# The second layer of a fused attention and bilinear MLP kernel: seven block products in place of eight

## The chip, the cores and the metric

The kernel runs on one core of a Trainium2 chip. The metric is device time in microseconds (us) of one launch; the times given are medians of several launches. Engines are called by the profile's names: PE (TensorE matmuls) and PEld (its weight loads), DVE (VectorE), ACT (ScalarE), POOL (GpSimd) and SP (SyncE, which here only issues transfers).

## The reference, cut to what matters

```python
def _attn_ref(q, k, v, w_pre, w_post):            # q, k, v: 4 x 12 x 448 x 64
    scores = np.matmul(q, k.transpose(0, 1, 3, 2)) / np.sqrt(64)
    scores = np.einsum('bhij,hg->bgij', scores, w_pre)
    attn = softmax(scores)                        # over the last axis
    attn = np.einsum('bhij,hg->bgij', attn, w_post)
    return np.matmul(attn, v)

def _moe_ref(x, w_a, w_b, w_out):                 # x: 1792 x 768, w_a, w_b: 768 x 1536, w_out: 1536 x 768
    return ((x @ w_a) * (x @ w_b)) @ w_out
```

The weights arrive as 64-bit floats and q, k, v as 32-bit floats; the result is float32.

## The kernel before

The attention takes the first 366 us or so and is not touched. Its result x stands transposed in DRAM, one block of 768 x 448 for each batch b (b = 0 to 3).

**First layer** (h = (x w_a) * (x w_b)), from about 366 to 705 us. The outer loop runs over f = 0 to 11, each f being 128 of the 1536 inner columns, and the inner loop over b. A step (f, b) is `run_a` and then `run_b`: each is 6 blocks of 128 rows of x, with three matmuls a block (high weights by high x, high weights by low x, low weights by high x; L583 to L585), since float32 is computed as sums of parts that the matmul takes in fp32r. `take_a` copies the first product from PSUM on ACT (L589), `take_b` multiplies the second by it on DVE into hf (L595) and stores hf to the DRAM tensor hd (L596, on SP, a step later).

In the same steps the weights of a later f, and those of the second layer, are converted from 64 to 32 bits: `bits` is six DVE instructions over 768 columns (L518 to L523) and one POOL addition (L524). For w_a and w_b, `split` then makes the high part on ACT (L561) and the low part on POOL (L562), into a pair of tiles wh and wl; for w_out, `conv_o` stores the converted block to the DRAM tensor wod (L550). `order` lists the conversions and `todo` says in which step (f, b) each runs.

**Second layer** (h w_out), from 705 us to the end. The loop runs over b and, inside it, over m = 0 to 5, the blocks of 128 output columns. A step j = (b, m) loads its weights from wod (`load_o`, two steps ahead), splits them (`split_o`: 2 ACT casts and 2 POOL subtractions of 768 columns), multiplies 12 blocks by three matmuls (`mm3`, L572 to L574), copies the result from PSUM on ACT with a change of order (L641 twice, L646) and stores it (L647). The h of the next b is loaded by three transfers at m = 0 (`load_h`, L624) and split at m = 2 to 5, 12 casts on ACT (L629) and 12 subtractions on DVE (L630). The first h is loaded after step (11, 1) of the first layer, and split in steps (11, 2) and (11, 3), six blocks each.

Instructions on an engine run in the order in which the program writes them, and SP issues its transfers in that order; buffers rotate inside a pool's tag (`bufs`). The tag `s` has two buffers (x of b = 0 and 1, later h), as has `pt` (attention weights, later x of b = 3 and h); PSUM products of the second layer take in turn `m` (three buffers) and `p0` or `p1` (one each).

Of the kernel before, what the change touches and what calls it, by code (L numbers as in the profile page):

```python
# [21 lines left out]
def talking_heads_bilinear_kernel(  # L22
# [20 lines left out]
    AB = 5  # L43
# [87 lines left out]
    def later(fn, n=3):  # L131
        todo_at.setdefault(now[0] + n, []).append(fn)
# [281 lines left out]
    for c in range(1, NC):  # L414
        b, t0, _ = chunks[c]
# [110 lines left out]

    def to_f32(u):
        t = raws.pop(u)
        n = mo["m"] = mo.get("m", -1) + 1
        m = (mo["w"] if n % 3 == 2 else mc).tile([128, CW], I32, tag="m", name="cvm", bufs=1 if n % 3 == 2 else 2)  # L530
        r = mc.tile([128, CW], I32, tag="r", name="cvr", bufs=1)
        return m.rearrange("p (k f) -> p k f", k=KD), bits(t[:, :, 0], t[:, :, 1], m, r)

    def conv_f(u):
# [7 lines left out]

        return ops, parts

    def conv_o(u):
        kind, i, e = u
        m, ops = to_f32(u)

        def store():
            nc.sync.dma_start(out=wod[:, i, e * KD:(e + 1) * KD], in_=m.bitcast(F32))  # L550

        return ops, lambda: later(store, 2)

    def load_o(j):
        if j < B * KD:
            raws["o", j] = raw_space().rearrange("p (k f) -> p k f", f=128)
            nc.sync.dma_start(out=raws["o", j], in_=wod[:, j % KD])

    def split(hh, ll, raw, e):
        sl = slice(e * KD, (e + 1) * KD)  # L560
        nc.scalar.copy(hh[:, sl], raw)  # L561
        nc.gpsimd.tensor_tensor(ll[:, sl], raw, hh.bitcast(F32)[:, sl], op=ALU.subtract)  # L562

    def split_o(j):
        hh, ll = new_w(("o", j))
        raw = raws.pop(("o", j))
        for e in range(2):
            split(hh, ll, raw[:, e * KD:(e + 1) * KD], e)

    def mm3(o, hh, ll, mh, ml, n, k0=0):  # L570
        for kk in range(n):
            nc.tensor.matmul(o, lhsT=hh[:, k0 + kk], rhs=mh[:, kk], start=(kk == 0), stop=False)  # L572
            nc.tensor.matmul(o, lhsT=hh[:, k0 + kk], rhs=ml[:, kk], start=False, stop=False)  # L573
            nc.tensor.matmul(o, lhsT=ll[:, k0 + kk], rhs=mh[:, kk], start=False, stop=(kk == n - 1))  # L574

    sas = {}

# [9 lines left out]
    def take_a(f, b, pa):  # L587
        sa = sb_p.tile([128, S], F32, tag="sb0", name="sa")
        nc.scalar.copy(sa, pa)  # L589
        sas[f, b] = sa  # L590

    def take_b(f, b, pb):
        sa = sas.pop((f, b))
        hf = w_p.tile([128, S], F32, tag="an", name="hf", bufs=AB)
# [8 lines left out]
    def run_b(f, b):  # L603
        pb = ps.tile([128, 512], F32, tag=f"p{b % 2}", name="pb", bufs=1)[:, :S]
        product(f, b, 1, pb, 0, KD)
        take_b(f, b, pb)
# [8 lines left out]
        if k1 == KD:  # L615
            (take_b if e else take_a)(0, 0, o)

    ht = {}

    def load_h(b):  # L620
        ll = big.tile([128, KF, S], F32R, tag="s" if b % 2 == 0 else "pt", name="hl")
        hh = big.tile([128, KF, S], F32R, tag="s" if b % 2 == 0 else "pt", name="hh")
        for f0, f1 in ((0, KF // 2), (KF // 2, KF - 1), (KF - 1, KF)):
            nc.sync.dma_start(out=ll.bitcast(F32)[:, f0:f1], in_=hd[b][:, f0:f1])  # L624
        ht[b] = (hh, ll)

    def split_h(b, f):
        hh, ll = ht[b]
        nc.scalar.copy(hh[:, f], ll.bitcast(F32)[:, f])  # L629
        nc.vector.tensor_tensor(ll[:, f], ll.bitcast(F32)[:, f], hh.bitcast(F32)[:, f], op=ALU.subtract)  # L630

    def run_o(j):
        b, m = divmod(j, KD)
        hh, ll = wt.pop(("o", j))
        th, tl = ht[b]
        po = ps.tile([128, 512], F32, tag="m" if j % 2 == 0 else f"p{j // 2 % 2}", name="po", bufs=3 if j % 2 == 0 else 1)[:, :S]
        mm3(po, hh, ll, th, tl, KF)
        so = sb_p.tile([128, S], F32, tag="sb1", name="so")
        n = S // QU * QU
        for e in range(2):  # L640
            nc.scalar.copy(  # L641
                so[:, :n].rearrange("p (u j e t) -> p u j e t", j=2, e=2, t=QH)[:, :, :, e],
                po[:, :n].rearrange("p (u e j t) -> p u e j t", j=2, e=2, t=QH)[:, :, e],
            )
        if n < S:
            nc.scalar.copy(so[:, n:], po[:, n:])  # L646
        nc.sync.dma_start(out=out[m * 128:(m + 1) * 128, b * S:(b + 1) * S], in_=so)  # L647

    order = [("f", f, e) for f in range(3) for e in range(2)] + [("o", 0, 0), ("o", 0, 1)]
    for f in range(2, KF):  # L650
# [86 lines left out]
    with tc.manual_schedule():  # L737
# [117 lines left out]
        fin3()  # L855
        todo = {(1, b): order[4 + b] for b in range(B)}
        for i, u in enumerate(order[8:]):
            todo[2 + i // 3, i % 3 if u[0] == "f" else 2] = u
        nxt = 6
        pairs = [(f, b) for f in range(1, KF) for b in range(B)]  # L860
        for i, (f, b) in enumerate(pairs):
            now[0] = 1000 + i
            for fn in todo_at.pop(now[0], ()):
                fn()
            if (f, b) in todo:
                ops, fin = conv(todo[f, b])
                for fn in ops:
                    fn()
                if nxt < len(order):
                    load_raw(order[nxt])[0]()  # L870
                    nxt += 1
            run_a(f, b)
            if (f, b) in todo:
                fin()
            run_b(f, b)
            if f == KF - 1 and b == 1:
                load_o(0)
                load_h(0)
                load_o(1)
                split_o(0)  # L880
            if f == KF - 1 and b > 1:
                for i in range(KF // 2 * (b - 2), KF // 2 * (b - 1)):
                    split_h(0, i)
            if b == B - 1:
                del wt["f", f]
        now[0] += 1
# [1 line left out]
            for fn in todo_at[t]:  # L888
                fn()
        todo_at.clear()  # L890
        for j in range(B * KD):
            b, m = divmod(j, KD)
            load_o(j + 2)
            if m == 0 and b + 1 < B:
                load_h(b + 1)
            if j + 1 < B * KD:
                split_o(j + 1)
            if b + 1 < B and m >= 2:
                for f in range(3 * (m - 2), 3 * (m - 1)):
                    split_h(b + 1, f)  # L900
            run_o(j)


# [46 lines left out]
```

## Time and profile before

| | |
|---|---|
| median of 3 runs | 894.05 us (893.24 to 895.97) |
| the profiled execution: span from its first to its last instruction | 883.4 us |
| what lies around the span, against the median | 10.65 us |
| PE busy, of the span | 98% |
| granted clock of TensorE, mean | 0.999 |

The page gives the profiled execution's own time as its span alone. "Busy" of an engine leaves out the issuing of transfers, and a matmul counts as busy for its whole way through the array, so that overlapping matmuls make PE look busier than it is: the distance from one matmul's start to the next tells more.

### The profile page before, as it was taken

What the parts mean: (1) busy time and instruction counts of PE and PEld (TensorE: products, weight loads), DVE (VectorE), ACT (ScalarE), POOL (GpSimd) and SP (SyncE); (2) the same over time, 40 slices, a digit from 0 to 9 for tenths busy, and PEclk for the clock granted to TensorE, in tenths of its full rate; (3) what the DMA queues carried; (4) which work ended last, traced back from release to release, by engine and by line L of the source; (5) the groups of instructions that cost most, each with busy time, mean ns of one, the idle gap of its engine ahead of it and who ended that gap; (6) DMA issues with size and microseconds to landing.
All of it is one profiled execution on the core that took longest, in us unless ns stands there. A gap on an engine that the chain in (4) does not pass through costs nothing.

```text
span 883.4 us, 27343 instructions
## 1 busy us (share of the span) xinstructions
PE 862.3 (98%) x11440; PEld 697.7 (79%) x11440; DVE 516.5 (58%) x913; ACT 376.8 (43%) x849; POOL 440.9 (50%) x549
## 2 busy tenths in 40 slices
PE   8799999999999899999999999999999999999998
PEld 4466566566566566899999999999999989999997
DVE  5577677667777685677755566555753545151500
ACT  5677677767677677431111111111111435353421
POOL 3786868587677762044432243233322255555552
PEclk9999999999999999999999999999999999999999
DMA  7776787676777964744433333333431674747441
GB/s 203 191 201 166 198 197 189 166 197 182 199 175 196 218 173 98 235 173 164 166 122 128 131 133 138 121 121 121 139 121 50 245 263 139 264 147 269 143 144 53
DMA packets 83172, 147.47 MB, mean 167 GB/s; under 512 B 42694, under 2 KB 63026, under 8 KB 82026
## 3 DMA queue, kind: packets, MB, share of 16 engines
q1 hardware_dynamic: 54922, 108.05, 37.9%
q0 software_dynamic: 28128, 37.68, 17.3%
q8 instruction: 90, 1.47, 0.7%
q14 instruction: 32, 0.26, 0.1%
HBM read 80.23 MB, written 26.74 MB: 121 GB/s over the span
## 4 chain that ended last, share of the span: by engine, by line
PE 91%; DMA 2%; DVE 2%; ACT 1%; issue 1%; SPq 1%; POOL 1%; ACTq 0%; DVEq 0%; POOLq 0%
PE pp L362 10%; PE xp L398 10%; PE mp L317 8%; PE pst L253 8%; PE po L573 6%; PE po L574 6%; PE po L572 6%; PE pa L583 6%; PE pa L585 6%; PE pa L584 6%; PE pb L585 6%; PE pb L584 6%; PE pb L583 6%; DMA sb<-s 1%; DMA k<-in_k_dram 1%
## 5 line engine op out<-in xcount | busy, mean ns | idle before, releaser
L297 POOL DMA_DIRECT2D sb<-s x350 | 202.1, 596 | 46.1 <-PE mp L317 22.0
L524 POOL TENSOR_TENSOR cvm<-cvm,cvr 128x768 int32<-128x768 int32 (+1 forms) x37 | 66.7, 1802 | 205.3 <-DVE cvm L523 205.3
L562 POOL TENSOR_TENSOR wl<-v,wh 128x768 fp32r<-128x768 f32 x48 | 93.4, 1966 | 100.7 <-ACT wh L561 100.7
L327 DVE TENSOR_REDUCE nm<-mp 124x1 f32<-124x448 f32 x180 | 104.0, 618 | 62.5 <-PE mp L317 61.7
L330 ACT ACTIVATE a<-mp,nm 124x448 f32<-124x448 f32 x180 | 112.7, 631 | 55.7 <-DVE nm L327 55.6
L398 PEld LDWEIGHTS xp<-pt,v 120*64 120x64 f32 x1536 | 74.0, 136 | 62.8 <-issue 45.1
L589 ACT COPY sa<-pa 128x448 f32<-128x448 f32 x47 | 25.2, 536 | 213.5 <-PE pa L585 210.2
L362 PE MATMUL pp<-kr,a 60*56 60x60 f32 x5760 | 102.0, 216 | 6.0 <-issue 5.3
L377 ACT COPY pt<-pp 120x480 f32<-120x480 f32 x176 | 91.3, 575 | 38.2 <-PE pp L362 37.8
L362 PEld LDWEIGHTS pp<-kr,a 60*56 60x56 f32 x5760 | 88.4, 127 | 23.0 <-issue 12.0
L573 PE MATMUL po<-hl,wh 128*128 128x448 f32 x288 | 104.5, 363 | 0.7 <-DVE hl L630 0.7
L574 PE MATMUL po<-hh,wl 128*128 128x448 f32 x288 | 104.4, 362 | 0.0
L572 PE MATMUL po<-hh,wh 128*128 128x448 f32 x288 | 104.4, 362 | 0.0
L585 PE MATMUL pb<-xhl,wl 128*128 128x448 f32 x282 | 102.3, 363 | 0.2 <-POOL wl L562 0.2
L583 PE MATMUL pb<-xhl,wh 128*128 128x448 f32 x282 | 102.2, 362 | 0.0
L584 PE MATMUL pb<-xhl,wh 128*128 128x448 f32 x282 | 102.2, 362 | 0.0
L595 DVE TENSOR_TENSOR hf<-pb,sa 128x448 f32<-128x448 f32 x47 | 29.4, 625 | 124.4 <-PE pb L585 118.8
L630 DVE TENSOR_TENSOR hl<-hl,hh 128x448 fp32r<-128x448 f32 x48 | 57.4, 1250 | 75.9 <-ACT hh L629 75.9
L317 PE MATMUL mp<-sb,wp 60*64 60x448 f32 x720 | 96.3, 543 | 3.1 <-DMA sb<-s 2.5
L253 PE MATMUL pst<-k,q 64*64 64x448 f32 x728 | 93.6, 540 | 4.8 <-ACT s L280 1.4
L583 PE MATMUL pa<-xhl,wh 128*128 128x448 f32 x264 | 95.7, 362 | 0.0
L584 PE MATMUL pa<-xhl,wh 128*128 128x448 f32 x264 | 95.7, 362 | 0.0
(94 smaller groups left out, 1400.1 us busy)
## 6 DMA issues: line engine op xcount, KB each, us to landing
sb<-s POOLq DMA_DIRECT2D x346, 105.0 KB, 4.9
v<-wod SPq DMA_DIRECT2D x24, 768.0 KB
v<-in_w_ab_dram SPq DMA_DIRECT2D x22, 768.0 KB
hd<-hf SPq DMA_DIRECT2D x48, 224.0 KB
v<-in_w_out_dram SPq DMA_DIRECT2D x12, 768.0 KB
v<-in_v_dram SPq DMA_DIRECT2D x48, 112.0 KB
xhl<-xd SPq DMA_DIRECT2D x24, 224.0 KB
hl<-hd SPq DMA_DIRECT2D x4, 1344.0 KB
```

Source lines behind the costliest of these rows:

```text
L253: nc.tensor.matmul(out[64 * e:64 * e + cols.stop - cols.start], lhsT=qt[c, i // QG][rows, i % QG, cols], rhs=kt[b, i][rows],)
L297: (nc.sync if u <= AH and i % 2 else nc.gpsimd).dma_start(out=sbt[u][i % 2][r:r + m * H], in_=rows)
L317: nc.tensor.matmul(mt[u, i // 2][col:col + M], lhsT=wp[r:r + m, :M], rhs=tiles[i % 2][r:r + m])
L330: nc.scalar.activation(a[:m], mp[:m], ACTF.Exp, bias=nm[:m], scale=1.0, accum_out=rss[u][:m, j:j + 1])
L362: nc.tensor.matmul(pp_t[i][64 * e:64 * e + C, H * r:H * r + H, j, :m], lhsT=a[rows, keys:keys + C], rhs=kr[rows, j, :, :m],)
L398: nc.tensor.matmul(xp[64 * e:64 * e + 64, p % 3, :n], lhsT=vt[b % 2][g][:C2, h % G, r], rhs=ptt[a][:C2, r, h, :n], start=(r == 0), stop=(r ...
L572: nc.tensor.matmul(o, lhsT=hh[:, k0 + kk], rhs=mh[:, kk], start=(kk == 0), stop=False)
L573: nc.tensor.matmul(o, lhsT=hh[:, k0 + kk], rhs=ml[:, kk], start=False, stop=False)
L574: nc.tensor.matmul(o, lhsT=ll[:, k0 + kk], rhs=mh[:, kk], start=False, stop=(kk == n - 1))
L583: nc.tensor.matmul(o, lhsT=hh[:, off + k], rhs=x[:, 0, k], start=first, stop=False)
L584: nc.tensor.matmul(o, lhsT=hh[:, off + k], rhs=x[:, 1, k], start=False, stop=False)
L585: nc.tensor.matmul(o, lhsT=ll[:, off + k], rhs=x[:, 0, k], start=False, stop=last)
```

## The change

The h of two neighbouring batches (a pair P = 0 or 1: b = 2P and 2P + 1) and the two halves of the 1536 inner columns make a 2 x 2 block matrix b11, b12, b21, b22; w_out makes one of a11, a12, a21, a22 from two neighbouring m (an m pair q = 0 to 2) and the same two halves. The second layer becomes seven products, in the order of the lists `OPS` and `HOPS`: a11 b11, a12 b21, s2 t2, s3 t3, s1 t1, s4 b22, a22 t4, with s1 = a21 + a22, s2 = s1 - a11, s3 = a11 - a21, s4 = a12 - s2, t1 = b12 - b11, t3 = b22 - b12, t2 = t3 + b11, t4 = t2 - b21. Each product runs over q and P (six groups of 6 blocks by three matmuls); `take_o` and `give` make the sums of the products on DVE, in a tile `acc`, and give out the results.

The sums s are made on POOL behind the conversion of w_out, in a tile `cw` of seven slots that takes a buffer of the tag `pt`; the sums t on POOL behind `take_b` of each odd b. For f = 6 to 11 the h of f - 6 is loaded back from DRAM for that (`reload_h`). All are stored to DRAM (`store_w`, `store_h`). The last conversion moves from step (11, 2) to (11, 0), and the first h loads stand behind (11, 0) and (11, 1).

```diff
-    hd = [dram.tile([128, KF, S], F32, name=f"hd{b}") for b in range(B)]
-    wod = dram.tile([128, KD, KF, 128], F32, name="wod")
+    hd = [dram.tile([128, len(OPS) + 1, KH2, S], F32, name=f"hd{b}") for b in range(B // 2)]
+    wod = dram.tile([128, len(OPS) * NQ, KH2 * 128], F32, name="wod")
...
     def conv_o(u):
...
+        def combine():
+            if x == "s1":
+                tt(slot("s3"), slot("a11"), slot("s1"), op=ALU.subtract)
+                later(lambda: store_w("s3", q), 2)
+                return
+            later(lambda: store_w(x, q), 2)
+            if x == "a22":
+                tt(slot("s1"), slot("s1"), slot("a22"), op=ALU.add)
+                tt(slot("s2"), slot("s1"), slot("a11"), op=ALU.subtract)
+                tt(slot("s4"), slot("a12"), slot("s2"), op=ALU.subtract)
+                for y in ("s1", "s2", "s4"):
+                    later(lambda y=y: store_w(y, q), 3)
...
     def split_o(j):
...
+        nc.scalar.copy(hh, raw)
+        nc.gpsimd.tensor_tensor(ll, raw, hh.bitcast(F32), op=ALU.subtract)
...
+    def reload_h(f, b):
+        for x in ("b11", "b12"):
+            t = back[x] = sb_p.tile([128, S], F32, tag="sb1", name="hr")
+            nc.sync.dma_start(out=t, in_=hd[b // 2][:, HOPS.index(x), f - KH2])
...
     def take_b(f, b, pb):
...
+        hf = hfs[b] = w_p.tile([128, S], F32, tag="an", name="hf", bufs=AB)
         nc.vector.tensor_tensor(hf, pb, sa, op=ALU.mult)
-        later(lambda: nc.sync.dma_start(out=hd[b][:, f], in_=hf), 1)
+        (P, e), (half, k) = divmod(b, 2), divmod(f, KH2)
+        later(lambda: store_h(P, f"b{half + 1}{e + 1}", k, hf), 1)
+        if half and not e:
+            reload_h(f, b)
+        if not e:
+            return
+        h0, tt = hfs[b - 1], nc.gpsimd.tensor_tensor
+        if not half:
+            t1 = sb_p.tile([128, S], F32, tag="sb1", name="t1")
+            tt(t1, hf, h0, op=ALU.subtract)
+            later(lambda: store_h(P, "t1", k, t1), 2)
+            return
+        t3, t2 = back.pop("b12"), back.pop("b11")
+        t4 = sb_p.tile([128, S], F32, tag="sb1", name="t4")
+        tt(t3, hf, t3, op=ALU.subtract)
+        tt(t2, t3, t2, op=ALU.add)
+        tt(t4, t2, h0, op=ALU.subtract)
+        for x, t in (("t3", t3), ("t2", t2), ("t4", t4)):
+            later(lambda x=x, t=t: store_h(P, x, k, t), 2)
...
+    def give(m, b, po, x, op):
         so = sb_p.tile([128, S], F32, tag="sb1", name="so")
...
         for e in range(2):
+            nc.vector.tensor_tensor(to[:, :, :, e], mix[0][:, :, e], mix[1][:, :, e], op=op)
         if n < S:
+            nc.vector.tensor_tensor(so[:, n:], ab[0][:, n:], ab[1][:, n:], op=op)
         nc.sync.dma_start(out=out[m * 128:(m + 1) * 128, b * S:(b + 1) * S], in_=so)
...
+    def take_o(i, q, P, po):
...
+        if i == 0:
+            nc.scalar.copy(x0, po)
+        elif i == 1:
+            give(2 * q, 2 * P, po, x0, ALU.add)
+        elif i == 2:
+            tt(x0, po, x0, op=ALU.add)
+        elif i == 3:
+            tt(x1, po, x0, op=ALU.add)
+        elif i == 4:
+            tt(x0, po, x0, op=ALU.add)
+            give(2 * q + 1, 2 * P + 1, po, x1, ALU.add)
+        elif i == 5:
+            give(2 * q, 2 * P + 1, po, x0, ALU.add)
+        else:
+            give(2 * q + 1, 2 * P, po, x1, ALU.subtract)
...
+        slot(OPS[0])
         load_x(3)
...
-            todo[2 + i // 3, i % 3 if u[0] == "f" else 2] = u
+            todo[2 + i // 3, i % 3 if u[0] == "f" else 2 * (2 + i // 3 < KF - 1)] = u
...
             run_b(f, b)
+            if f == KF - 1 and b == 0:
+                load_h(0, 0)
             if f == KF - 1 and b == 1:
                 load_o(0)
-                load_h(0)
+                load_h(0, 1)
                 load_o(1)
                 split_o(0)
...
-        for j in range(B * KD):
...
+        load_h(1, 0)
+        SPLIT_AT = (0, 2, 4, 7, 9, 12)
+        R6 = 2 * NQ
+        for n in range(NP * 2):
+            i, r = divmod(n, R6)
+            if n % 2 == 0:
+                load_o(n // 2 + 2)
+                if n // 2 + 1 < NP:
+                    split_o(n // 2 + 1)
+            if r == 0:
+                load_h(i + 1, 1)
+            for f in range(SPLIT_AT[r - 1] if r else 0, SPLIT_AT[r]):
+                split_h(i + 1, *divmod(f, KH2))
+            run_o(n)
+            if r == R6 - 2 and i + 2 <= len(OPS):
+                load_h(i + 2, 0)
```

## Rows read from the trace of the kernel before

**Rows 1.** The page: span, engines, granted clock by fortieths, chain by engine.

```profile
span 883.4 us, 27343 instructions
...
PE 862.3 (98%) x11440; PEld 697.7 (79%) x11440; DVE 516.5 (58%) x913; ACT 376.8 (43%) x849; POOL 440.9 (50%) x549
...
PEclk9999999999999999999999999999999999999999
...
PE 91%; DMA 2%; DVE 2%; ACT 1%; issue 1%; SPq 1%; POOL 1%; ACTq 0%; DVEq 0%; POOLq 0%
```

**Rows 2.** Busy times by stretch: first layer in halves, one b of the second.

```profile
core 0: us, PE busy (x) PEld busy (x) DVE busy (x) ACT busy (x) POOL busy (x), PEclk, DMA share, GB/s
388.00:546.80 158.80, 158.56 (x793) 148.46 (x792) 102.64 (x130) 21.85 (x34) 57.32 (x31) 1.00 0.39 137
546.80:705.50 158.70, 158.70 (x796) 148.92 (x795) 87.79 (x112) 26.48 (x45) 49.07 (x26) 1.00 0.37 134
...
748.70:791.90 43.20, 43.20 (x218) 40.54 (x217) 15.62 (x13) 18.49 (x42) 23.49 (x12) 1.00 0.57 206
```

**Rows 3.** PE in order of time: start of the second layer, its stall, the end.

```profile
705.47 0.36 PE L572 MATMUL po<-hh,wh 128*128 128x448 f32 x1
...
710.27 0.36 PE L572 MATMUL po<-hh,wh 128*128 128x448 f32 x1
711.30 0.47 PE L573 MATMUL po<-hl,wh 128*128 128x448 f32 x1 [0.67 <-DVE hl L630]
...
879.03 0.36 PE L574 MATMUL po<-hh,wl 128*128 128x448 f32 x1
```

**Rows 4.** What PE waited for from 330 us to the end.

```profile
PE po L573 <- DVE hl L630: 0.7, 1, 0.7
...
PE pb L585 <- POOL wl L562: 0.2, 1, 0.2
```

**Rows 5.** Groups of instructions from 700 us to the end.

```profile
L562 POOL TENSOR_TENSOR wl<-v,wh 128x768 fp32r<-128x768 f32 x46 | 89.4, 1964 | 80.9 <-ACT wh L561 80.9
L630 DVE TENSOR_TENSOR hl<-hl,hh 128x448 fp32r<-128x448 f32 x48 | 57.4, 1250 | 75.9 <-ACT hh L629 75.9
...
L641 ACT COPY so<-po 128x220 f32<-128x220 f32 x48 | 14.8, 366 | 106.6 <-PE po L574 106.6
```

**Rows 6.** DVE and POOL in order of time, end of the first layer.

```profile
699.07 3.94 DVE L630 TENSOR_TENSOR hl<-hl,hh 128x448 fp32r<-128x448 f32 x6
705.73 0.62 DVE L595 TENSOR_TENSOR hf<-pb,sa 128x448 f32<-128x448 f32 x1 [2.72 <-ACT hh L629]
706.26 0.61 DVE L630 TENSOR_TENSOR hl<-hl,hh 128x448 fp32r<-128x448 f32 x1
...
706.43 2.16 POOL L562 TENSOR_TENSOR wl<-v,wh 128x768 fp32r<-128x768 f32 x1 [6.58 <-ACT wh L561]
...
708.54 2.22 POOL L562 TENSOR_TENSOR wl<-v,wh 128x768 fp32r<-128x768 f32 x1
```

**Rows 7.** Shortest, median and longest of hl, wl and hf (ns).

```profile
L630 DVE TENSOR_TENSOR hl<-hl,hh x48: 610/1184/2269, 699.1 to 835.0; 128x448 fp32r<-128x448 f32 x48
...
L595 DVE TENSOR_TENSOR hf<-pb,sa x47: 615/625/625, 374.7 to 705.7; 128x448 f32<-128x448 f32 x47
```

**Rows 8.** DVE, POOL and PE where f = 1 begins.

```profile
388.42 0.62 DVE L595 TENSOR_TENSOR hf<-pb,sa 128x448 f32<-128x448 f32 x1 [0.89 <-PE pb L585]
388.96 0.91 DVE L518 TENSOR_SCALAR cvm<-v 128x768 int32<-128x768 int32 x1
...
387.60 1.84 POOL L524 TENSOR_TENSOR cvm<-cvm,cvr 128x768 int32<-128x768 int32 x1 [4.01 <-DVE cvm L523]
390.39 2.11 POOL L562 TENSOR_TENSOR wl<-cvm,wh 128x768 fp32r<-128x768 f32 x1 [0.95 <-ACT wh L561]
...
392.55 0.47 PE L585 MATMUL pb<-xhl,wl 128*128 128x448 f32 x1 [0.24 <-POOL wl L562]
```

**Rows 9.** A stretch in which x is loaded by transfers of 224 KB.

```profile
375.00:380.00 5.00, 5.00 (x27) 4.69 (x26) 1.78 (x4) 2.45 (x6) 1.75 (x1) 1.00 0.95 318
```

More of the change, by code (lines that the diff above doesn't have):

```diff
@@ L51, in talking_heads_bilinear_kernel @@
     KH = KD // 2
+    KH2 = KF // 2
+    NQ = KD // 2
+    OPS = ("a11", "a12", "s2", "s3", "s1", "s4", "a22")
+    HOPS = ("b11", "b21", "t2", "t3", "t1", "b22", "t4", "b12")
+    NP = len(OPS) * NQ
     AH = 4
@@ L543, in conv_f, with slot, store_w @@
         return ops, parts
+    cw = {}
+    def slot(x):
+        if not cw:
+            cw["t"] = big.tile([128, len(OPS), CW], F32, tag="pt", name="cw")
+        return cw["t"][:, OPS.index(x)]
+    def store_w(x, q):
+        nc.sync.dma_start(out=wod[:, OPS.index(x) * NQ + q], in_=slot(x))
     def conv_o(u):
         kind, i, e = u
[L547 to L552, printed above, removed]
+        q, row = divmod(i, 2)
+        x = ("a11", "a12", "s1", "a22")[2 * row + e]
+        t = raws.pop(u)
+        r = mc.tile([128, CW], I32, tag="r", name="cvr", bufs=1)
+        ops = bits(t[:, :, 0], t[:, :, 1], slot(x).bitcast(I32), r)
+        tt = nc.gpsimd.tensor_tensor
+        def combine():
[10 more added lines that the diff above has]
+                    later(lambda y=y: store_w(y, q), 3)
+        return ops, combine
     def load_o(j):
-        if j < B * KD:
-            raws["o", j] = raw_space().rearrange("p (k f) -> p k f", f=128)
-            nc.sync.dma_start(out=raws["o", j], in_=wod[:, j % KD])
+        if j < NP:
+            raws["o", j] = raw_space()[:, :CW]
+            nc.sync.dma_start(out=raws["o", j], in_=wod[:, j])
     def split(hh, ll, raw, e):
@@ L564, in split_o @@
     def split_o(j):
[L565 to L574, printed above, removed]
+        hh, ll = wt["o", j] = [mo["w"].tile([128, KH2, 128], F32R, tag=x, name=x) for x in ("wh", "wl")]
+        raw = raws.pop(("o", j)).rearrange("p (k f) -> p k f", f=128)
+        nc.scalar.copy(hh, raw)
+        nc.gpsimd.tensor_tensor(ll, raw, hh.bitcast(F32), op=ALU.subtract)
     sas = {}
@@ L590, in take_a, with store_h @@
         sas[f, b] = sa
+    hfs, back = {}, {}
+    def store_h(P, x, k, t):
+        nc.sync.dma_start(out=hd[P][:, HOPS.index(x), k], in_=t)
+    def reload_h(f, b):
+        for x in ("b11", "b12"):
+            t = back[x] = sb_p.tile([128, S], F32, tag="sb1", name="hr")
+            nc.sync.dma_start(out=t, in_=hd[b // 2][:, HOPS.index(x), f - KH2])
     def take_b(f, b, pb):
         sa = sas.pop((f, b))
[L594 removed]
+        hf = hfs[b] = w_p.tile([128, S], F32, tag="an", name="hf", bufs=AB)
         nc.vector.tensor_tensor(hf, pb, sa, op=ALU.mult)
[L596 removed]
+        (P, e), (half, k) = divmod(b, 2), divmod(f, KH2)
[17 more added lines that the diff above has]
+            later(lambda x=x, t=t: store_h(P, x, k, t), 2)
     def run_a(f, b):
@@ L616, in part_of @@
             (take_b if e else take_a)(0, 0, o)
[L618 to L637, printed above, removed]
+    ht, acc = {}, {}
+    def load_h(i, P):
+        if i == len(OPS):
+            return
+        t = ht[i, P] = big.tile([128, 2, KH2, S], F32R, tag="s" if i % 2 == 0 else "pt", name="hhl")
+        for f in range(0, KH2, 2):
+            nc.sync.dma_start(out=t.bitcast(F32)[:, 1, f:f + 2], in_=hd[P][:, i, f:f + 2])
@@ L638, in run_o, with split_h @@
+    def split_h(i, P, f):
+        if i == len(OPS):
+            return
+        t = ht[i, P]
+        raw, hf = t.bitcast(F32)[:, 1, f], t.bitcast(F32)[:, 0, f]
+        nc.scalar.copy(t[:, 0, f], raw)
+        nc.vector.tensor_tensor(t[:, 1, f], raw, hf, op=ALU.subtract)
+    def give(m, b, po, x, op):
         so = sb_p.tile([128, S], F32, tag="sb1", name="so")
         n = S // QU * QU
+        ab = (x, po) if op == ALU.subtract else (po, x)
+        mix = [t[:, :n].rearrange("p (u e j t) -> p u e j t", j=2, e=2, t=QH) for t in ab]
+        to = so[:, :n].rearrange("p (u j e t) -> p u j e t", j=2, e=2, t=QH)
@@ L647, in run_o @@
         nc.sync.dma_start(out=out[m * 128:(m + 1) * 128, b * S:(b + 1) * S], in_=so)
+    def take_o(i, q, P, po):
+        if not acc:
+            acc["t"] = mo["x"].tile([128, 2, B // 2, NQ, S], F32, tag="x", name="acc")
+        x0, x1 = acc["t"][:, 0, P, q], acc["t"][:, 1, P, q]
+        tt = nc.vector.tensor_tensor
+        if i == 0:
[13 more added lines that the diff above has]
+            give(2 * q + 1, 2 * P, po, x1, ALU.subtract)
@@ new lines, in run_o @@
+    def run_o(n):
+        (i, q), P = divmod(n // 2, NQ), n % 2
+        hh, ll = wt["o", n // 2]
+        t = ht[i, P]
+        po = ps.tile([128, 512], F32, tag="m" if n % 2 == 0 else f"p{n // 2 % 2}", name="po", bufs=3 if n % 2 == 0 else 1)[:, :S]
+        for k in range(KH2):
+            nc.tensor.matmul(po, lhsT=hh[:, k], rhs=t[:, 0, k], start=(k == 0), stop=False)
+            nc.tensor.matmul(po, lhsT=hh[:, k], rhs=t[:, 1, k], start=False, stop=False)
+            nc.tensor.matmul(po, lhsT=ll[:, k], rhs=t[:, 0, k], start=False, stop=(k == KH2 - 1))
+        if P:
+            del wt["o", n // 2]
+        take_o(i, q, P, po)
@@ L881, in talking_heads_bilinear_kernel @@
             if f == KF - 1 and b > 1:
-                for i in range(KF // 2 * (b - 2), KF // 2 * (b - 1)):
-                    split_h(0, i)
+                for i in range(KH2):
+                    split_h(0, b - 2, i)
             if b == B - 1:
```

15 lines of the change are left out of this document (removed).

## The prediction

> **What bounds the kernel now.** I read the page first [rows 1]: PE is busy for 98% of the span, the chain that ended last is PE for 91%, and the granted clock is at its upper level (2.4 GHz) in every fortieth. Since overlapping matmuls flatter PE's busy time, I then took the distance between starts. The second layer has 4 x 6 x 12 x 3 = 864 matmuls; the first starts at 705.47 us and the last at 879.03 us [rows 3], so 863 distances take 173.56 us. One stall lies in them: at 711.30 us, 1.03 us behind the matmul before, where 0.20 is usual, so 0.83 us lost. (173.56 - 0.83) / 863 = 0.2002 us a matmul. The view of waits says the same from the other side: behind the attention PE waited twice, for the low part of h and for a low part of weights [rows 4]. So from 366 us on, time is the number of matmuls times 0.2002 us, plus stalls.
>
> The view by stretch shows what the change may fill [rows 2]. In the first layer DVE is busy 65% and then 55%, POOL 36% and then 31%, the DMA engines 37 to 39%; in one b of the second layer (43.2 us) DVE 36%, ACT 43%, POOL 54%, DMA 57%. A third reading is how DVE and POOL meet: the DVE subtraction of 448 columns takes 0.61 us alone, six in a row 3.94 us, but 1.25 us on the mean and up to 2.27 us [rows 5, 6, 7], and two POOL subtractions that take turns with it stretch from 1.85 to 2.2 us [rows 6]. Each waits for the other's whole instruction, one for one. The multiplication in `take_b`, which reads PSUM, never shows that: 0.615 to 0.625 us in all 47 [rows 7].
>
> **The change, part by part.**
>
> *Removed.* Seven products of 3 m pairs x 2 batch pairs x 6 blocks x 3 = 108 matmuls are 756, for 864: 108 x 0.2002 = **-21.6 us**, if PE stays fed.
>
> *Seam at the second layer's start.* Before, six DVE subtractions stand behind the last `take_b`, at 706.26 us, 0.79 us after the first matmul, and alternate with two POOL subtractions; that made the 0.83 us stall [rows 3, 6]. After, POOL first makes t3, t2, t4 for step (11, 3), as soon as hf is there (0.88 us), and then one weight split. POOL's nearest row is the addition of 768 columns, 1.84 us [rows 8]; by columns a sum of 448 is 1.84 x 448 / 768 = 1.08 us. With turns one for one the six DVE subtractions then end at about 1.4, 2.95, 4.5, 6.1, 8.4 and 9.0 us. They are the h of P = 1, read by the second group of 18 matmuls, which starts at 3.6 us and wants one each 0.6 us from 3.8 us on: the fourth is 0.5 us late and the fifth 1.7 us more. 2.2 us for 0.83 before: **+1.4 us**. Bounds: no stall at all (-0.8), if POOL stays behind DVE; and, if a sum of 448 columns takes as long as one of 768, 5.5 us of stall (+4.7). The h loads themselves now start a step (7.2 us) sooner and were not what was late.
>
> *Seam at f = 1.* The low part of its second half of weights is already late by 0.4 us at 392.55 us [rows 8]. A t1 sum (step (0, 3)) is now in front of it on POOL: the addition ends at 389.44 us, DVE's waiting instruction goes first, then t1 to about 390.95, one more DVE instruction, and the split ends at about 393.3 in place of 392.5: **+0.8 us**. Bounds 0 (t1 fits into POOL's 0.95 us of idle time) and +1.8 (a sum of 1.84 us).
>
> *Other new sums in the first layer.* 12 t1 and 36 of t2, t3, t4 at 1.08 us are 52 us, 12 sums of w_out at 1.84 us are 22 us. Most of it falls on f = 6 to 11 (172.8 us): 36 x 1.08 + 8 x 1.84 = 54 us on top of about 53 already there, so POOL is busy some 62%. DVE, at 88 us of 158.7 or 96 of 172.8, can be held for the same 54 us at most: 150 us, 87%. It will run late inside an f and catch up in step (f, 3), which has no conversion. What is behind a late DVE: the multiplication in `take_b`, and by it the PSUM buffer p0 or p1. That is wanted again 1.5 steps later, 10.8 us; I work out DVE's worst lag (f = 7, three sums of w_out on POOL) as 5 to 7 us. Weights are split a step or two ahead of their f. **0 us**; bound +3, one such lag running over in f = 7 and f = 11.
>
> *SP and transfers.* SP gets 48 more h stores, 24 reloads and 9 more weight stores: about 20 MB over 317 us, 62 GB/s on top of 135 [rows 2], and in f = 6 to 11 about 90 on top of 134. Transfers of the same small size moved 318 GB/s [rows 9]. The t stores are issued two steps behind the sums and find them done. In the last flush SP waits for t4 (about 5.6 us after the second layer's start) and holds up the load of b21 and of the third weights: these are wanted at 21.6 and at 14.4 + 2 us, and 1.7 MB at 318 GB/s is 5.4 us. **0 us**.
>
> *Second layer, per product (21.6 us).* DVE takes 12 subtractions instead of 12 in 43.2 us, and the results: `give` is three instructions, which I put at 0.38, 0.38 and 0.16 us (columns of the 0.62 us row; ACT's row for the same 220 columns is 0.37 [rows 5]). Of POOL's splits there is one per 7.2 us, three per product, where before two stood there. Each can hold one subtraction for 1.85 us: 12 x 0.61 + 3 x 1.85 = 12.9 us, and the fullest product, s1 t1, adds 6 x (0.62 + 0.92) = 9.2: 22.1 us, 0.5 over; by the mean of 1.25 us, 24.2, 2.6 over. The next product adds 5.5 only, and PSUM covers a lag of 10.8 us again (p0 and p1 in turn). **0 us**; bound +2.6. ACT: 12 casts, three of weights, at most six copies, some 13 us. Transfers: 2.75 MB of h, 1.18 of weights, up to 1.38 of results, 5.3 MB in 21.6 us or 246 GB/s, below 318.
>
> The Trainium skill (DMA: Bandwidth & Descriptors, Bandwidth) speaks against this part: it asks for at least 1 MiB per transfer if three quarters of the peak rate are wanted. Its fit for one transfer from GpSimd's queue (Anatomy of one DMA), 2.0 us + bytes / 436 GB/s, makes an h piece of 448 KB 3.05 us, weights of 384 KB 2.9 and a result of 224 KB 2.5, by estimate; one at a time, six, three and six of them would be some 42 us a product, and the second layer would be paced by transfers. The rate in rows 9, with pieces of 224 KB from SP, says that they overlap; no run here shows the fit itself. The sum stands without it.
>
> *Moved, and the end.* The tile `cw` takes the buffer of `pt` that x of b = 3 had; x then waits for the other one, which the last attention matmuls free before its data is stored. 0. The last result goes out by DVE in place of ACT: 0.
>
> **Sum.** -21.6 + 1.4 + 0.8 = -19.4 us. The span of 883.4 us becomes 864.0; with the 10.65 us between span and median unchanged, 894.05 becomes 874.6.
>
> **The rivals.**
>
> *DVE and POOL in each other's way cost more than two seams.* For it: DVE at 87% in f = 6 to 11, by my bound, and instructions held to 2.27 us. Against: every wait has 7 to 10 us of slack. It gives back the other bounds: 4.7 + 1.8 + 3 + 2.6 for 2.2 at most, +9.9 us, so 878 to 884.5 us.
>
> *The second layer is paced by DVE: no faster, or slower.* The place is its in-order queue, subtractions and results. It decides from 25.2 us per product (21.6 + 21.6 / 6, six products having splits): gain gone. With 4.6 us of results on the mean of those six that needs (25.2 - 4.6) / 12 = 1.72 us a subtraction; slower by 0.3% needs 1.75. For it: 2.27 us occurs. Against: the mean was 1.25 with twice as many POOL splits. At 1.85 us, each held for a POOL split's length: 26.8 x 6 + 21.6 = 182.4 us for 173.6 before, about 903 us.
>
> *The second layer is paced by transfers.* For it: it moved 206 GB/s before, and the pieces are a third as long. If 206 were all it can have, a product takes 5.3 / 206 = 25.7 us and the gain is gone: about 895 us. Against: 206 was what was asked for, at 57% of the DMA engines, and 318 GB/s is in the same trace [rows 2, 9].
>
> **How the numbers follow.** Forecast 0.72; the first rival 0.17; paced by DVE 0.05; paced by transfers 0.04; something I don't see, slower, 0.02. Best case -22.4 us, 871.6; my own bounds alone reach 884.5, but all of them at once is unlikely, and half of the added 9.9 us ends at 879.5. A range of 871.5 to 880 leaves out the second half of the first rival and the others, about 2 in 10. A measurement of this kernel tells 0.3%, 2.7 us, from no change. The forecast and the first rival are faster; of the transfer-paced case, the DVE-paced one and the unseen one, 0.11 together, I give 0.04 to no change and 0.06 to slower, 0.01 to faster.
>
> **What would show it.** Right: distances of 0.20 us throughout the 756 matmuls; a stall of about 2 us for the low part of h in the second group of 18; the stall at f = 1 near 1.2 us; `take_b` still 0.62 us and never followed by a PE wait. Wrong: PE waiting for DVE at the start of each product (DVE-paced), for casts behind an h load (transfers), or for p0 or p1 in f = 7 and 11. The whole is wrong if sums of 448 columns on POOL take much more than 1.1 us, or if POOL, held behind a late reload, brings the weights of f + 1 too late.

## The result, and the profile after

The changed kernel takes 883.62 us (median of 4 runs, 880.08 to 887.57), the kernel before 895.01 us (4 runs, 893.24 to 899.41): ratio 0.988, 95% interval 0.984 to 0.993. It is faster by 1.2%, 10 to 11 us, a little over half of the 19.4 us that the prediction summed, and 883.62 lies above its range of 871.5 to 880. The ratios, here and below, leave out runs that lie more than 1.5% above the fastest of their kernel; the medians hold all runs.

The page of the changed kernel, lines that answer to [rows 1]:

```profile
span 885.9 us, 27500 instructions
...
PE 855.7 (97%) x11332; PEld 679.6 (77%) x11332; DVE 596.1 (67%) x1039; ACT 362.4 (41%) x792; POOL 479.4 (54%) x582
...
PEclk9999999999999999999999999999999999999999
...
PE 89%; DVE 3%; issue 2%; DMA 2%; ACT 2%; POOL 1%; SPq 1%; DVEq 0%; ACTq 0%; POOLq 0%
```

Its 108 matmuls are gone (11440 to 11332), and yet the span is 2.5 us longer than that of [rows 1]. The profiled execution took 887.57 us, 1.7 us more than its span. So the 10.65 us that the prediction put "around the span" were mostly something else: if 1.7 us lie around the span there too, the profiled execution of before was about 9 us faster than the median of its runs.

PE in order of time, the lines that answer to [rows 3] and, first, to the end of [rows 8]:

```profile
403.53 0.36 PE L607 MATMUL pb<-xhl,wh 128*128 128x448 f32 x1
403.73 0.36 PE L608 MATMUL pb<-xhl,wh 128*128 128x448 f32 x1
404.82 0.47 PE L609 MATMUL pb<-xhl,wl 128*128 128x448 f32 x1 [0.73 <-POOL wl L592]
405.13 0.36 PE L607 MATMUL pb<-xhl,wh 128*128 128x448 f32 x1
...
600.01 0.37 PE L608 MATMUL pb<-xhl,wh 128*128 128x448 f32 x1
600.22 0.37 PE L609 MATMUL pb<-xhl,wl 128*128 128x448 f32 x1
600.43 0.37 PE L607 MATMUL pb<-xhl,wh 128*128 128x448 f32 x1
...
728.15 0.37 PE L726 MATMUL po<-hhl,wh 128*128 128x448 f32 x1
...
734.19 0.47 PE L727 MATMUL po<-hhl,wh 128*128 128x448 f32 x1
...
736.35 0.47 PE L727 MATMUL po<-hhl,wh 128*128 128x448 f32 x1 [1.28 <-DVE hhl L685]
...
881.07 0.36 PE L727 MATMUL po<-hhl,wh 128*128 128x448 f32 x1
881.27 0.36 PE L728 MATMUL po<-hhl,wl 128*128 128x448 f32 x1
```

Three things stand here. At f = 1 the distance of two starts is 1.09 us, where [rows 8] has 0.60. Behind it the matmuls start 0.207 us apart, not 0.200: 600.01, 600.22, 600.43. And the second layer, from 728.15 to 881.27, has its two gaps near the start, and 0.200 us again behind them, up to its end: 881.07, 881.27.

The instructions of the first products from f = 1 on, by tile (shortest, median, longest in ns, then first and last start):

```profile
L607 PE MATMUL pa<-xhl,wh x264: 362/368/368, 399.9 to 723.8; 128*128 128x448 f32 x132
```

The same 264 matmuls took 323.9 us from the first to the last; in the second trace of the kernel before, shown below, they took 313.1. A matmul's own duration is 368 ns in place of 362: in this view the slower distance is seen at once.

By stages, each from the start of its first matmul (the first layer from the first step behind the attention; the last matmul's 0.2 us counts to the second layer):

| | before, us | after, us | difference |
|---|---|---|---|
| attention, up to step (0, 1) | 366.4 | 378.2 | +11.8 |
| first layer | 339.0 | 349.9 | +10.9 |
| second layer | 173.8 | 153.3 | -20.5 |
| end | 4.2 | 4.4 | +0.2 |

The attention has the same instructions in both kernels; in the traces of this case it took 366.4 to 378.2 us, so its 11.8 us are a difference of two executions. The second layer gave what was summed for it. The first layer took half of that back.

Busy times by stretch, as [rows 2]: the second half of the first layer, and two products of the second, a12 b21 and s1 t1:

```profile
core 0: us, PE busy (x) PEld busy (x) DVE busy (x) ACT busy (x) POOL busy (x), PEclk, DMA share, GB/s
...
563.90:728.10 164.20, 164.20 (x796) 148.86 (x795) 117.48 (x112) 25.51 (x44) 111.36 (x66) 1.00 0.62 214
...
751.87:773.47 21.60, 21.60 (x109) 20.29 (x108) 13.00 (x27) 8.55 (x16) 5.55 (x3) 1.00 0.62 214
...
816.67:838.27 21.60, 21.60 (x110) 20.30 (x108) 15.95 (x33) 8.11 (x15) 5.55 (x3) 1.00 0.60 207
```

The granted clock is at its upper level in all of them, so the 0.207 us are not the clock. The second of these products is the one in which DVE is busiest of those behind the start, and it has 5.65 us of 21.6 left; the transfers have 30% or more of the time left: neither DVE nor the transfers pace the second layer.

### The profile page after: what moved, and what is told of

Same layout as the page of the kernel before. It is cut to its first block, busy times and chain, and to the rows that moved or that the text cites. A ratio compares the mean times of both kernels' runs of the same rounds, so it can differ in the third digit from the quotient of the medians.

```text
span 885.9 us, 27500 instructions
## 1 busy us (share of the span) xinstructions
PE 855.7 (97%) x11332; PEld 679.6 (77%) x11332; DVE 596.1 (67%) x1039; ACT 362.4 (41%) x792; POOL 479.4 (54%) x582
## 4 chain that ended last, share of the span: by engine, by line
PE 89%; DVE 3%; issue 2%; DMA 2%; ACT 2%; POOL 1%; SPq 1%; DVEq 0%; ACTq 0%; POOLq 0%
PE pp L367 9%; PE xp L403 9%; PE pst L258 8%; PE mp L322 7%; PE pa L607 6%; PE pa L609 6%; PE pa L608 6%; PE pb L609 6%; PE pb L607 6%; PE pb L608 6%; PE po L727 5%; PE po L728 5%; PE po L726 5%; DVE hhl L685 1%; SPq L302 1%
## 5 line engine op out<-in xcount | busy, mean ns | idle before, releaser
L367 PE MATMUL pp<-kr,a 60*56 60x60 f32 x5760 | 103.9, 216 | 14.6 <-issue 14.0
L367 PEld LDWEIGHTS pp<-kr,a 60*56 60x56 f32 x5760 | 89.5, 127 | 32.8 <-issue 21.6
L607 PE MATMUL pb<-xhl,wh 128*128 128x448 f32 x282 | 103.6, 367 | 0.0
L608 PE MATMUL pb<-xhl,wh 128*128 128x448 f32 x282 | 103.6, 367 | 0.0
L529 POOL TENSOR_TENSOR cvm<-cvm,cvr 128x768 int32<-128x768 int32 (+1 forms) x25 | 44.4, 1775 | 98.5 <-DVE cvm L528 98.5
L609 PE MATMUL pa<-xhl,wl 128*128 128x448 f32 x264 | 97.0, 368 | 0.0
L607 PE MATMUL pa<-xhl,wh 128*128 128x448 f32 x264 | 97.0, 368 | 0.0
L608 PE MATMUL pa<-xhl,wh 128*128 128x448 f32 x264 | 97.0, 368 | 0.0
L403 PE MATMUL xp<-pt,v 120*64 120x120 f32 (+1 forms) x1536 | 93.8, 265 | 1.2 <-ACT pt L382 0.6
L727 PE MATMUL po<-hhl,wh 128*128 128x448 f32 x252 | 91.7, 364 | 1.4 <-DVE hhl L685 1.3
L598 POOL TENSOR_TENSOR wl<-v,wh 128x768 fp32r<-128x768 f32 x21 | 39.2, 1867 | 98.9 <-ACT wh L597 98.9
L728 PE MATMUL po<-hhl,wl 128*128 128x448 f32 x252 | 91.5, 363 | 0.0
```

What stands on the lines that cost most here:

```text
L367: nc.tensor.matmul(pp_t[i][64 * e:64 * e + C, H * r:H * r + H, j, :m], lhsT=a[rows, keys:keys + C], rhs=kr[rows, j, :, :m],)
L403: nc.tensor.matmul(xp[64 * e:64 * e + 64, p % 3, :n], lhsT=vt[b % 2][g][:C2, h % G, r], rhs=ptt[a][:C2, r, h, :n], start=(r == 0), stop=(r ...
L607: nc.tensor.matmul(o, lhsT=hh[:, off + k], rhs=x[:, 0, k], start=first, stop=False)
L608: nc.tensor.matmul(o, lhsT=hh[:, off + k], rhs=x[:, 1, k], start=False, stop=False)
L609: nc.tensor.matmul(o, lhsT=ll[:, off + k], rhs=x[:, 0, k], start=False, stop=last)
L727: nc.tensor.matmul(po, lhsT=hh[:, k], rhs=t[:, 1, k], start=False, stop=False)
```

## The experiments

Theory 1, formed from this trace: behind a stall PE's matmuls run on at 0.200 or at 0.207 us, and stay so until another stall. Theory 2: the sums that the change adds to the first layer slow each matmul. The trace speaks for theory 1 (f = 0 at 0.200, 0.207 from the stall at f = 1 to the gap at 736 us), but one trace can't tell what one more execution would show.

**Both kernels once more.** No edit.

> The kernel before, unchanged, for a second trace. Theory 1 (a stall of PE can leave the matmuls of the stretch behind it 0.207 us apart in place of 0.200, and only another stall ends that; which of the two comes out is settled at the stall, and can differ from run to run): the distance is one of these two values in each layer, constant from stall to stall, perhaps not the 0.200 us of the first trace; where it is 0.207 us, that layer is 3.3% longer (first layer +10.6 us, second +5.8 us). Theory 2 (the sums that the change adds slow each matmul of the first layer, by contention): 0.200 us in both layers. Both: a ratio near 1.00.

> The changed kernel, unchanged, for a second trace. Theory 1: the distance between matmuls is 0.200 or 0.207 us, constant between stalls, and it changes only at a stall; the first layer may come out at either. Theory 2: 0.207 us again from f = 1 to 11, since the same sums run. Both: the second layer at 153 us or close to it, 756 matmuls and some 2 us of stall.

The kernel before: ratio 1.002 (0.996 to 1.007), first layer 339.0 us, second 173.8, the same stalls to 0.01 us. The changed kernel: ratio 0.980 (0.973 to 0.987), first layer 339.5 us, second 153.7. PE of this second trace of the changed kernel at f = 1:

```profile
401.48 0.47 PE L609 MATMUL pb<-xhl,wl 128*128 128x448 f32 x1 [0.73 <-POOL wl L592]
401.79 0.37 PE L607 MATMUL pb<-xhl,wh 128*128 128x448 f32 x1
401.99 0.36 PE L608 MATMUL pb<-xhl,wh 128*128 128x448 f32 x1
402.19 0.36 PE L609 MATMUL pb<-xhl,wl 128*128 128x448 f32 x1
```

and its matmuls by tile, below them those of the second trace of the kernel before:

```profile
L607 PE MATMUL pa<-xhl,wh x264: 362/362/363, 396.6 to 710.2; 128*128 128x448 f32 x132
```

```profile
L583 PE MATMUL pa<-xhl,wh x264: 362/362/363, 397.9 to 711.0; 128*128 128x448 f32 x132
```

The stall is the same (idle 0.73 us, a distance of 1.09), the sums are the same, and behind it the distance is 0.200. That ends theory 2 as it was put: one program, two executions, two distances.

**The stall at f = 1 shortened.** The low part of the weights goes in front of the t1 sum, in two halves.

```diff
     run_a(0, 3)
     ops3, fin3 = conv(order[3])
     run(ops3)
-    run_b(0, 3)
-    fin3()
+    fin3(2)          # the low part in two instructions of 384 columns
+    run_b(0, 3)
```

> The changed kernel, but the low part of the second half of the weights of f = 1 is made in front of the t1 sum of step (0, 3), in two instructions of 384 columns, so that PE should not wait at f = 1. All sums stay. Theory 1: no stall there, so nothing throws the matmuls out of step; 0.200 us from f = 0 to 11, the first layer 10 to 11 us shorter than in the trace of the changed kernel, ratio to before about 0.976. Theory 2: 0.207 us as before the edit, and only the stall of 0.9 us is gone.

A distance of 0.45 us is left there, 0.200 us behind it, first layer 338.9 us, second 153.4; ratio 0.979 (0.971 to 0.987).

**One sum in the kernel before.** Nothing of the change but one POOL instruction.

```diff
     run_b(0, 3)
+    t1 = sb_p.tile([128, S], F32, tag="sb1", name="t1")
+    nc.gpsimd.tensor_tensor(t1, hfs[3], hfs[2], op=ALU.subtract)
     fin3()
```

> The kernel before with one POOL subtraction of 128 x 448 added (its result is not used), where the change has the t1 sum of step (0, 3): behind the last multiplication of f = 0 and in front of the low part of the weights of f = 1. Nothing else. Theory 1: the stall at f = 1 grows from 0.4 to 0.9 us or so, as in the changed kernel, and may leave 0.207 us behind it for the rest of the first layer, +10 us from one instruction. Theory 2: the stall grows by 0.5 us and that is all; 0.200 us behind it, ratio 1.000 to 1.001.

> The kernel before with the one POOL subtraction at f = 1, a second time. Theory 1: the same stall of 1.1 us, and 0.200 or 0.207 us behind it as the restart falls. Rival (that instruction always brings 0.207): the first layer at 349.9 us again.

Its matmuls by tile, first trace:

```profile
L583 PE MATMUL pa<-xhl,wh x264: 362/367/368, 395.1 to 719.0; 128*128 128x448 f32 x132
```

The stall is a distance of 1.10 us, and the first layer takes 349.9 us: 10.9 us more from one instruction of 1.48 us, whose result nobody reads and which holds up PE once. Over its runs it is slower than before by 1.0% (ratio 1.010, 1.003 to 1.016). The stall of the second layer's start, 0.88 us in this trace, ends it: 173.8 us. In the second trace the stall is 1.38 us, the distance behind it 0.200, the first layer 339.8. So the sums of the change are not needed for it, and the instruction doesn't always bring it. Nor does the chip decide: the first of these traces (0.207) and the second trace of the changed kernel (0.200) are from one chip.

**A stall in each f.** In the kernel before, the low part of one weight block of each f from 2 to 11 waits for two small POOL instructions behind `take_a`.

```diff
     run_a(f, b)
+    if f in kept and b == 0:
+        release(f, b)    # z = sa - sa; low part of the first block = kept[f] + z
```

> The kernel before with a small stall of PE put into each f from 2 to 11: the low part of the first block of the second half of the weights is released only behind two small POOL instructions that wait for the copy of the first product of step (f, 0). By the rows of the changed kernel PE then waits some 1.3 us at even f and 1.7 at odd f. Theory 1 (the distance is drawn at each restart): some of the ten stretches of 28.8 us run at 0.207 us and the others at 0.200, in no order, each constant up to the next stall; by the five stalls of about 1.1 us or less at f = 1 seen so far two to four of ten, and where the first gap behind the restart is 306 ns rather than 310 or 311. Rival (the place at f = 1, or the sums, make it): all ten at 0.200.

It missed what it was for. The small instructions stood behind a conversion's addition on POOL, the distances at nine of the ten stalls were 3.8 to 4.2 us, and the granted clock fell to its lower level (1.2 GHz) around each of these (matmuls 0.373 us apart); at the tenth, 1.90 us, it did not. The eighth stall, and the second layer by tile:

```profile
668.88 0.74 PE L602 MATMUL pb<-xhl,wl 128*128 128x448 f32 x1 [3.84 <-POOL wl L541]
...
L589 PE MATMUL po<-hh,wh x288: 358/368/368, 763.4 to 942.2; 128*128 128x448 f32 x144
```

Behind the first seven stalls the distance is 0.200 once the clock is back up; behind the eighth it is 0.207, and stays that through two stalls more, that of the second layer's start (0.88 us) and the second layer, 179.3 us. So a later stall need not end it. No sum of the change is in this kernel and nothing was put in at f = 1, so neither is needed; but with the clock down at most restarts, it can't count how often a short stall brings 0.207.

**The stall at f = 1 taken away, and that of the second layer's start.**

```diff
     run_a(0, 2)
+    ops3, fin3 = conv(order[3])
+    run(ops3[:2])
     run(split_all(3))
...
+    if f == KF - 1 and b == 3:
+        for i in range(KH2):
+            split_h(0, 1, i)
     run_b(f, b)
```

> As the run without most of the stall at f = 1, and two edits more: the first two instructions of the last conversion of f = 0 go in front of the split of x of b = 3, which should take the rest of the stall at f = 1; and the last six subtractions of the first h (P = 1) go in front of the last multiplication of the first layer on DVE, so that they do not take turns with the three sums on POOL. Theory 1: no stall behind the attention, 0.200 us in both layers, first layer 338.4 us, second 151.3 to 151.6 in place of 153.4 to 153.7; about 2.5 us less than the changed kernel at its better distance and 13 less than at its worse. Rival: the second layer's start waits for something else (weights or the h of the second product) and stays at 153 us.

> The changed kernel, unchanged, for a third trace and beside the run without stalls on one chip. Theory 1: first layer 339.5 us or 349.9, second 153.3 to 153.7; ratio to before 0.976 to 0.990 as the draws fall.

On one chip: without the stalls 867.76 us, ratio 0.973 (0.968 to 0.979); the changed kernel 872.83, ratio 0.978 (0.973 to 0.983), its trace 340.0 and 153.4 us. No stall at f = 1, first layer 338.5 us. The second layer still took 152.8: the rival was right, something stood behind the first stall. What PE waited for, from 370 us to the end:

```profile
PE po L731 <- POOL wl L601: 1.2, 1, 1.2
```

Its POOL in order of time:

```profile
710.52 1.15 POOL L647 TENSOR_TENSOR hr<-hf,hr 128x448 f32<-128x448 f32 x1 [9.55 <-DMA hd<-t]
711.75 1.16 POOL L648 TENSOR_TENSOR hr<-hr 128x448 f32<-128x448 f32 x1
712.98 1.16 POOL L649 TENSOR_TENSOR t<-hr,hf 128x448 f32<-128x448 f32 x1
714.10 1.83 POOL L601 TENSOR_TENSOR wl<-v,wh 128x768 fp32r<-128x768 f32 x1
723.40 1.81 POOL L601 TENSOR_TENSOR wl<-v,wh 128x768 fp32r<-128x768 f32 x1 [7.46 <-ACT wh L600]
```

and its SP, the stores of the last sums, the load of b21, and that of the third weights (v<-wod):

```profile
711.70 1.55 SPq L622 DMA_DIRECT2D hd<-hr  x2
714.16 0.50 SPq L622 DMA_DIRECT2D hd<-t  x1
714.77 1.47 SPq L680 DMA_DIRECT2D hhl<-hd  x3
716.28 0.43 SPq L587 DMA_DIRECT2D v<-wod  x1
```

Read from below: the third weights were issued at 716.28 us, behind the stores of t3, t2 and t4, and POOL could split them from 723.40 on. In the changed kernel the stall before it hid that, all but 0.2 us (a distance of 0.42 us at 731.59 in its second trace). With DVE out of the way each of the three sums takes 1.15 us.

**The third weights in front of the last stores.**

```diff
             if f == KF - 1 and b == 2:
+                load_o(2)
```

> As the run without stalls, with the load of the third weights of the second layer issued behind step (11, 2), in front of the last stores of the first layer in SP's queue. In that run PE waited 1.4 us for these weights, which landed 6 us after their issue. My theory of the second layer's start (its stalls were the low part of h, then these weights, and nothing stands behind them): no stall above 0.4 us, 151.2 to 151.5 us for the second layer, about 863 to 866 us, the fastest so far. Rival (the h of the second product is next): another stall of about 1 us in the first two products, 152.5 us.

> As the run with the third weights loaded early, but with f = 1 as the changed kernel has it: the low part of the second half of its weights behind the t1 sum on POOL, one stall of 1.1 to 1.6 us. Both runs differ by that stall alone. Theory 1: the difference of the medians is 1.0 us if no run falls to 0.207 us behind it, and up to 11.5 us if all do; between them it tells in how many runs it does. In the trace the first layer is 339.5 to 340.0 or 349.9 us. Rival (the stall costs its own length and no more): 1.0 to 1.5 us.

PE of the first of the two, start and end of the second layer:

```profile
713.68 0.36 PE L729 MATMUL po<-hhl,wh 128*128 128x448 f32 x1
...
864.68 0.36 PE L731 MATMUL po<-hhl,wl 128*128 128x448 f32 x1
```

151.0 us for 755 distances, 0.2000 each, no stall at all behind the attention: 338.5 and 151.2 us. Its 870.97 us (ratio 0.978, 0.974 to 0.982) are not below the 867.76 of the run before on another chip, and not the 863 to 866 expected: in its trace the attention took 375.2 us, there 370.5.

The run that differs by the stall at f = 1 alone has a median of 874.34 us (0.979, 0.975 to 0.983), 3.4 us more, five runs of 870.6 to 876.5 and one of 885.96, the traced one:

```profile
L726 PE MATMUL po<-hhl,wh x252: 367/367/368, 723.7 to 879.3; 128*128 128x448 f32 x126
```

349.9 and 156.2 us: with no stall left that could end it, 0.207 us went on through the second layer.

**The changed kernel and the best version, side by side.**

> The changed kernel, unchanged, a fourth trace, beside the best version on one chip. Theory 1: behind the stall of 1.1 to 1.6 us at f = 1 the first layer at 339.5 to 340.0 us or at 349.9, the second at 153.3 to 153.7; the median 0.976 to 0.981 of before if most runs stay at 0.200 us, 0.987 to 0.989 if most fall to 0.207.

> The version with neither stall and the third weights loaded early, again. Theory 1: no stall, 338.5 and 151.2 us, in this trace as in the last; 3.5 us (1.1 + 2.3) below the changed kernel where that stays at 0.200 us, and 13 to 14 us below it where it falls to 0.207; the spread of its runs is that of the attention alone.

Changed: 879.52 us, 0.982 (0.977 to 0.987); its six runs fall into 874.2 to 877.6 and 881.4 to 885.0, and the traced one, 885.01, has 349.9 us in the first layer behind a stall of 1.10 us. Best: 866.15 us, six runs from 863.3 to 868.4, 338.6 and 151.2 us, ratio 0.969 (0.965 to 0.973). It beats both kernels: 3.1% below before.

**Does the length of the stall decide?** The one sum in the kernel before again, with other lengths (448 + 112 and 448 + 224 columns in two instructions).

```diff
-    nc.gpsimd.tensor_tensor(t1, hfs[3], hfs[2], op=ALU.subtract)
+    nc.gpsimd.tensor_tensor(t1[:, :224], hfs[3][:, :224], hfs[2][:, :224], op=ALU.subtract)
```

> The kernel before with the added POOL subtraction at f = 1 cut to 224 columns. Theory 1a (the length of the stall decides: about 1.1 us brings 0.207 us, others do not): a stall of 0.8 us, 0.200 us behind it, first layer 339.3 us. Theory 1b (any restart can): either.

> The same with 336 columns. Theory 1a: a stall of 0.95 us, 0.200 us behind it. Theory 1b: either.

> The same with 448 and 112 columns in two instructions. Theory 1a: a stall of 1.4 to 1.9 us, 0.200 us behind it, first layer 340.0 us. Theory 1b: either.

> The same with 448 and 224 columns in two instructions. Theory 1a: a stall of 1.6 to 2.2 us, 0.200 us behind it. Theory 1b: either.

Distances at the stall of 1.03, 2.10, 1.78 and 2.80 us, longer and less even than expected, and 0.200 us behind each. But in the third of them the usual stall of the second layer's start (1.03 us, the length that left 0.200 in other traces) left 0.207:

```profile
L572 PE MATMUL po<-hh,wh x288: 360/367/368, 710.9 to 889.6; 128*128 128x448 f32 x144
```

179.3 us for 173.8. The length does not decide. This trace also shows both distances in one execution, and that the kernel before, which has this same stall, may draw 0.207 too: its two traces don't, but its untraced runs on one chip lie between 887.4 and 914.0 us. All traces (distance at f = 1, first and second layer; the run with ten stalls left out):

| kernel | at f = 1, us | first layer | second layer |
|---|---|---|---|
| before, twice | 0.60, 0.60 | 339.0, 339.0 | 173.8, 173.8 |
| changed, four times | 1.09, 1.09, 1.55, 1.10 | 349.9, 339.5, 340.0, 349.9 | 153.3, 153.7, 153.4, 153.3 |
| one sum in before, twice | 1.10, 1.38 | 349.9, 339.8 | 173.8, 173.8 |
| its lengths 224, 336, 560, 672 | 1.03, 2.10, 1.78, 2.80 | 339.5, 340.5, 340.2, 341.2 | 173.8, 173.8, 179.3, 173.8 |
| stall at f = 1 shortened | 0.45 | 338.9 | 153.4 |
| stall at f = 1 alone | 1.08 | 349.9 | 156.2 |
| no stalls; weights early, twice | none | 338.5; 338.5, 338.6 | 152.8; 151.2, 151.2 |

## Why the prediction was wrong

The step that failed is the first: "time is the number of matmuls times 0.2002 us, plus stalls". It took the distance behind a stall for a constant. The seam at f = 1 was priced at +0.8 us; the stall grew by 0.49 us, and what followed it cost 10.4 us more in four of the eleven traces in which the distance there is above 1 us. The slowdown is shown by those traces, and so is that neither the sums nor a certain length of the stall make it. One of the four timed runs is the traced one, which had it. That the other three had it too is only argued: their spans, 878.4 to 882.5 us, less 507.6 us (349.9 + 153.3 + 4.4) leave 370.8 to 374.9 for the attention, inside the 366.4 to 378.2 of the traces; less 497.2 they would leave 381.2 to 385.3, which no trace shows. A longer attention can't be ruled out, though: the slowest run with the one sum in the kernel before, a span of 916.3 us, leaves some 383 for it even with 0.207 us in both layers. In the later comparisons, with both distances seen in the traces, the changed kernel came to 0.980, 0.978 and 0.982 of before, a gain of 16 to 20 us by these ratios, for 19.4 of the sum; no one comparison is the prediction's proof, but the terms can be checked one by one.

*The matmuls removed.* Right. -20.5 us in the second layer against -21.6 + 1.4 = -20.2.

*The second layer's start.* Its size was right, 2.1 to 2.5 us above 151.2 for 2.2 predicted, and its cause too: DVE's subtractions taking turns with three sums and a split on POOL. In the trace it is two waits, at the fourth and the fifth block of the second group, of which the second (1.65 us between starts) is the long one, as the working had it. What I put at 0, SP held up by t4 in front of the third weights, was late as well, by 1.4 us, and was hidden behind that stall. I had taken the landing for the end of it and left out the cast and the split behind it: in the run without stalls the weights landed at about 722.4 us, the split ended at 725.2, and PE wanted the low part at 723.9.

*The sums.* POOL, lines of the changed kernel from 375 us to the end:

```profile
L592 POOL TENSOR_TENSOR wl<-cvm,wh 128x768 fp32r<-128x768 f32 x22 | 45.7, 2076 | 23.2 <-ACT wh L591 23.2
...
L645 POOL TENSOR_TENSOR hr<-hr 128x448 f32<-128x448 f32 x12 | 18.1, 1505 | 0.9
...
L639 POOL TENSOR_TENSOR t<-hf 128x448 f32<-128x448 f32 x12 | 16.9, 1412 | 19.1 <-DVE hf L629 19.1
```

1.41 to 1.50 us against 1.08, the turns with DVE included; 1.15 without. In f = 6 to 11 of the second trace, which has 0.200 us as the sum had it (columns as in the stretches above):

```profile
541.59:714.39 172.80, 172.80 (x865) 162.16 (x864) 131.03 (x126) 27.45 (x47) 117.06 (x69) 1.00 0.63 218
```

POOL is busy 68% of it (62 predicted), DVE 76% (87 was my bound). The multiplication of `take_b` began up to 4.7 us behind PE's last matmul in the second trace of the changed kernel, where I had put 5 to 7; PE never waited for it. The sums were put some 35% too short, and the cost of 0 us was right all the same. The stores of the sums, which the working expected to be "done" when SP comes to them, were not: SP waited for POOL in front of them, up to 4.2 us at once in the first trace. PE waited for none of it but the third weights.

*The rivals.* None came. DVE is busy 16.0 us in s1 t1, which the working had as the fullest at 22.1 (the first product, with its stalls, has 17.6 of 23.7), the transfers at most 71% of the time, and PE runs through all products but the first without a wait.

*The time.* The 10.65 us between span and median were 1.7 us around the span and some 9 us by which that execution was faster. It cancels in the difference, but it shows that one trace of this kernel is one draw out of a range of more than 20 us, and the prediction's range had no term for that. Nor did four runs tell 0.3%, as it has it: the interval of the ratio is 0.984 to 0.993.

## What to carry to other kernels

Before a kernel's time is written as instructions times a distance, look at whether that distance is the same in two traces of it, and behind each stall. Here a stall of 1 us on a stream of 1,600 matmuls could cost 11, so it was worth more to remove the two short stalls than their length says: without them the six runs of the last comparison lay within 5.1 us, and the version was 13 us faster than the changed kernel. On another chip, where the changed kernel's trace had 0.200, the version without the stalls (the third weights not yet early) was 5 us faster. When a stall is removed, look at once for the wait that it hid; and a load that is wanted early goes in front of the stores that wait for the last sums in the same queue.

## What the runs showed of the hardware that was not expected

Dense 128 x 128 by 448 matmuls, each with its own weight load, run at 0.200 or at 0.207 us from start to start at the same granted clock, and stay at one of them for hundreds of microseconds. The change from one to the other was only ever seen at a stall: to 0.207 behind distances of 1.03 to 1.10 us, and once behind 4.20 us; back to 0.200 behind 0.88 and 1.65. Behind most other stalls, distances of 0.42 to 2.80 us, up to seven matmuls run at 0.201 to 0.209 and then 0.200 again.

One mark goes with it, which the run with ten stalls had been expected to test and couldn't, its clock being down. The first matmul behind the stall at f = 1 is the longest of its tile, and lasts 468 ns in the four traces with 0.207 behind it and 470 to 472 in the other seven; the changed kernel's first and second trace:

```profile
L609 PE MATMUL pb<-xhl,wl x282: 362/368/468, 382.3 to 727.9; 128*128 128x448 f32 x141
```

```profile
L609 PE MATMUL pb<-xhl,wl x282: 362/362/471, 379.0 to 714.2; 128*128 128x448 f32 x141
```

In nanoseconds, the second matmul starts 306 behind the first at each of these four and where the run with 448 + 112 columns fell to 0.207; at no other stall of the 18 traces (distances above 0.4 us) is it 306: it is 305, or 307 and more. So a few nanoseconds at the restart go with what follows. Five cases don't show that they decide it. What inside PE this is, and what decides it, stays open.
